# Softmax denominators by block transposes on VectorE in place of DMA, and the MLP of a batch directly behind its attention

## The chip, the cores and the metric

The kernel runs on one core of one Trainium2 chip. The metric is the device time of one execution in microseconds (us), the median of several runs. A core has TensorE (matrix products, the profile's PE; its weight loads are PEld), VectorE (DVE), ScalarE (ACT), GpSimd (POOL) and SyncE (SP, which here only starts transfers). Each engine works through its own queue in order. Queues wait for one another by semaphores.

## The reference, cut to what matters

```python
# B, H, S, D = 8, 8, 576, 64;  d_model = 512, d_ff = 2048
scores = q @ k.T / sqrt(D) + decay            # decay from cumulative log f
scores = where(causal, -1e9, scores)
attn   = softmax(scores);  o = attn @ v       # per batch and head
x = o.transpose(0, 2, 1, 3).reshape(B * S, H * D)
out = gelu_tanh(x @ w_in) @ w_out
```

The kernel works on transposed scores, so the softmax denominator of a query comes out of the attn-V product as one more output row: extra columns of the stationary operand hold the decay weights. Four heads are one item, and a batch has two items.

## The kernel before

The parts (cuts marked):

```python
psS: 2 tiles of 2 PSUM banks    # scores, and up-projection
psO: 1 tile of 2 PSUM banks     # po, attn-V of one head
psM: 2 tiles of 1 PSUM bank     # pso, down-projection

def attn_out(i, h):
    po = psO.tile([128, 1024], FP32)
    # ... 9 matmuls: 64 rows of numerator, and a denominator row in the other half
    nc.vector.tensor_copy(oT[i % 2][:, h, :], po[:, 256:256 + S])

def den_load(i, h):     # DMA: the denominator row to 16 partitions
def den_spread(i, x):   # reciprocal, DMA to DRAM, DMA broadcast to rb (64 rows per head)
def scale_out(i, x):
    for y in range(2):  # GpSimd, half the partitions each
        nc.gpsimd.tensor_mul(xT[b % 3][s, ...], oT[i % 2][s, 2 * x + y, :], rb[s, :])

def mask(i, r):         # VectorE: causal mask on the diagonal blocks of round r
    nc.vector.tensor_mul(p[...], p[...], utri)

def step(i, j, old, fill, per_round, n=None, out_first=False):
    for r in range(4):
        score_round(i, r)              # TensorE, then exponentials on ScalarE
        attn_out(j, r); den_load(j, r)
        # ... GpSimd casts, VectorE transposes of q and k, den_spread, scale_out
        if r > 0: mask(i, r - 1)
        pull(fill, per_round)          # held down-projection matmuls
        if r == 3: mask(i, 3)          # ...

for b in range(3, B + 1):
    mlp_in(b - 2, ...)                 # up-projection of an older batch
    # ...
    for i in (2 * b, 2 * b + 1):
        step(i, i - 1, i - 2, fill, held // 8, ...)
```

Every step has the scores of one item beside the attn-V of the item before it, and held down-projection matmuls in each round. Attention runs more than one batch ahead of the MLP.

The softmax here doesn't subtract the row's maximum and nothing guards it: scores larger than these inputs give would overflow.

## Time and profile before

| quantity | before |
|---|---|
| time, median of 4 runs | 428.88 us |
| span of the profiled run | 425.9 us |
| first long up-projection burst starts at | 60.0 us |
| second starts at | 136.2 us |
| two steady batches (136.16 to 224.89) | 88.73 us, TensorE busy 84.02 |

The first lines of the profile page give the span, and each engine's busy time and instruction count:

```profile
span 425.9 us, 7272 instructions
PE 355.0 (83%) x2825; PEld 210.9 (50%) x2825; DVE 160.7 (38%) x263; ACT 204.0 (48%) x274; POOL 177.7 (42%) x159
```

The waits view, TensorE only. Each line says who waited for whom: total us, times, longest us.

```profile
PE ps_h L253 <- POOL xT_100 L245: 17.3, 5, 5.5
PE ps_h L253 <- POOL xT_101 L245: 13.2, 1, 13.2
...
PE po L206 <- DVE pt_96 L194: 4.1, 5, 1.1
PE po L206 <- DVE oT_98 L213: 3.5, 1, 3.5
```

The up-projection (L253) loses 32 us to normalised attention output that comes late (a third line, of 1.6 us, is not shown), all but 3.5 us of it before 136 us. Behind those GpSimd multiplies stand the transfers of the denominators: row load, store and broadcast.

From there on TensorE sets the pace: it is busy for 84.02 of the next 88.73 us. One attention round in the timeline (start us, duration us, engine, line, what):

```profile
259.35 0.57 PE L176 MATMUL ps_s<-qT_91,kT_93 32*128 32x448 bf16 x8
259.86 0.86 PE L206 MATMUL po<-pt_96,v_aug_94 128*128 128x256 bf16 x7
260.55 2.11 PE L270 MATMUL pso<-w_out_sb,gT 128*128 128x512 bf16 x9
260.82 0.76 DVE L213 COPY oT_98<-po 128x576 f32<-128x576 f32 x1 [1.55 <-PE po L206]
261.50 0.73 DVE L194 TENSOR_TENSOR pt_97<-pt_97,utri 128x512 bf16<-128x512 bf16 x1
262.59 0.52 PE L176 MATMUL ps_s<-qT_91,kT_93 32*128 32x320 bf16 x16
```

Scores, attn-V and held matmuls follow one another without a hole.

### The profile page before, as it was taken

To read this page: it belongs to the slowest core of one execution; us is meant where nothing else is said; L and a number is where in the kernel's file an instruction comes from. 1 tells how busy PE (TensorE), PEld (TensorE's weight loads), DVE (VectorE), ACT (ScalarE), POOL (GpSimd) and SP (SyncE) were. 2 spreads that over 40 slices of the span, in tenths; PEclk is the share of its full clock that TensorE was granted. 3 is DMA by queue.
4 is the path that set the end of the run, shared out by engine and by line. 5 is a ranking of instruction groups with operands and counts; after the bars stand their busy time and mean duration, and the time that the engine had idled before them with its cause. 6 is when DMAs were issued, how large, how long until landed. Compare 5 with 4: busy or idle time off the path is not lost.

```text
span 425.9 us, 7272 instructions
## 1 busy us (share of the span) xinstructions
PE 355.0 (83%) x2825; PEld 210.9 (50%) x2825; DVE 160.7 (38%) x263; ACT 204.0 (48%) x274; POOL 177.7 (42%) x159
## 2 busy tenths in 40 slices
PE   0577149878806999999889999999899989999996
PEld 0234027434403754575447644764476445766642
DVE  6285301274502136531743164505630774000021
ACT  2656116745301664567545745575557551643300
POOL 2491583242805605770568054812881553600000
PEclk9968659899876999999999999999999999999999
DMA  9999179966771971289137922594310132301021
GB/s 194 219 200 181 60 162 199 204 124 154 178 151 70 230 153 69 79 193 195 55 107 190 199 79 83 156 195 116 108 53 2 56 107 83 83 0 51 25 75 74
DMA packets 94642, 52.31 MB, mean 123 GB/s; under 512 B 44880, under 2 KB 85840, under 8 KB 94608
## 3 DMA queue, kind: packets, MB, share of 16 engines
q1 hardware_dynamic: 87952, 46.47, 46.6%
q0 software_dynamic: 4224, 4.19, 6.2%
q10 hardware_dynamic: 2432, 1.18, 1.4%
q8 instruction: 22, 0.36, 0.4%
q14 instruction: 12, 0.10, 0.1%
HBM read 46.28 MB, written 9.58 MB: 131 GB/s over the span
## 4 chain that ended last, share of the span: by engine, by line
PE 55%; DMA 8%; DVE 6%; issue 4%; SPq 3%; ACT 3%; POOL 1%; DVEq 0%; POOLq 0%; ACTq 0%
PE ps_h L253 26%; PE pso L270 20%; PE po L206 6%; DMA rb<-rrow 3%; PE ps_s L176 3%; DMA rrow<-den 3%; DVE pt_96 L194 2%; ACT pt_96 L185 2%; SPq L116 2%; DVE pt_97 L194 1%; DVE oT_99 L213 1%; DMA den<-oT_98 1%; SPq L104 1%; ACT L185 1%; POOL xT_100 L245 1%
## 5 line engine op out<-in xcount | busy, mean ns | idle before, releaser
L270 PE MATMUL pso<-w_out_sb,gT 128*128 128x512 bf16 x576 | 138.5, 384 | 0.0
L260 ACT ACTIVATE gT<-ps_h 128x576 bf16<-128x576 f32 x128 | 83.2, 650 | 112.8 <-PE ps_h L253 112.8
L253 PEld LDWEIGHTS <-w_in_sb 128*128 128x128 bf16 x1024 | 101.4, 99 | 65.6 <-issue 33.5
L270 PEld LDWEIGHTS <-gT 128*128 128x128 bf16 x576 | 53.2, 99 | 60.5 <-issue 7.7
L185 ACT ACTIVATE pt_97<-ps_s 128x800 bf16<-128x800 f32 (+3 forms) x64 | 50.1, 834 | 48.4 <-PE ps_s L176 40.6
L253 PE MATMUL ps_h<-xT_100,w_in_sb 128*128 128x288 bf16 x384 | 50.8, 294 | 17.3 <-POOL xT_100 L245 17.3
L185 ACT ACTIVATE pt_96<-ps_s 128x800 bf16<-128x800 f32 (+3 forms) x64 | 50.1, 834 | 30.7 <-PE ps_s L176 21.1
L253 PE MATMUL ps_h<-xT_101,w_in_sb 128*128 128x288 bf16 x384 | 51.6, 290 | 13.2 <-POOL xT_101 L245 13.2
L213 DVE COPY oT_99<-po 128x576 f32<-128x576 f32 x32 | 24.1, 753 | 86.9 <-PE po L206 86.8
L274 DVE COPY o_st<-pso 128x512 f32<-128x512 f32 x36 | 24.5, 680 | 70.7 <-PE pso L270 70.5
L213 DVE COPY oT_98<-po 128x576 f32<-128x576 f32 x32 | 24.2, 755 | 39.9 <-PE po L206 39.6
L206 PE MATMUL po<-pt_96,v_aug_94 128*128 128x320 bf16 (+4 forms) x224 | 31.9, 281 | 8.0 <-DVE pt_96 L194 4.1
L206 PE MATMUL po<-pt_97,v_aug_95 128*128 128x320 bf16 (+4 forms) x224 | 29.3, 268 | 5.2 <-DVE pt_97 L194 2.8
L253 PE MATMUL ps_h<-xT_102,w_in_sb 128*128 128x288 bf16 x256 | 32.2, 286 | 1.6 <-POOL xT_102 L245 1.6
L245 POOL TENSOR_TENSOR xT_100<-oT_98,rb 64x576 bf16<-64x576 f32 x12 | 17.2, 1436 | 37.8 <-DMA rb<-rrow 37.3
L245 POOL TENSOR_TENSOR xT_101<-oT_98,rb 64x576 bf16<-64x576 f32 x12 | 16.9, 1408 | 33.6 <-DMA rb<-rrow 28.1
L176 PE MATMUL ps_s<-qT_90,kT_92 32*128 32x400 bf16 (+5 forms) x384 | 22.1, 295 | 10.3 <-DVE kT_92 L137 4.6
L206 PEld LDWEIGHTS <-v_aug_94 128*128 128x128 bf16 x224 | 19.0, 103 | 17.9 <-issue 13.6
L194 DVE TENSOR_TENSOR pt_97<-pt_97,utri 128x512 bf16<-128x512 bf16 (+1 forms) x40 | 27.3, 711 | 0.0
L206 PEld LDWEIGHTS <-v_aug_95 128*128 128x128 bf16 x224 | 18.8, 99 | 15.6 <-issue 11.3
L245 POOL TENSOR_TENSOR xT_101<-oT_99,rb 64x576 bf16<-64x576 f32 x12 | 17.0, 1413 | 22.3 <-DMA rb<-rrow 18.6
L194 DVE TENSOR_TENSOR pt_96<-pt_96,utri 128x512 bf16<-128x512 bf16 (+1 forms) x40 | 25.7, 671 | 0.0
(59 smaller groups left out, 236.0 us busy)
## 6 DMA issues: line engine op xcount, KB each, us to landing
rb<-rrow SPq DMA_DIRECT2D x64, 144.0 KB, 3.0
out_dram<-o_st SPq DMA_DIRECT2D x36, 256.0 KB, 2.2
k_nat_84<-in_k_dram SPq DMA_DIRECT2D x32, 144.0 KB, 4.4
k_nat_85<-in_k_dram SPq DMA_DIRECT2D x32, 144.0 KB, 4.5
v_nat_88<-in_v_dram SPq DMA_DIRECT2D x16, 256.0 KB, 6.3
v_nat_89<-in_v_dram SPq DMA_DIRECT2D x16, 256.0 KB, 5.9
q_nat_82<-in_q_dram SPq DMA_DIRECT2D x28, 144.0 KB, 4.7
q_nat_83<-in_q_dram SPq DMA_DIRECT2D x28, 144.0 KB, 5.2
```

Of the source, the lines that this page charges most:

```text
L104: eng.dma_start(out=dst[i % 2][32 * h:32 * h + 32].rearrange("p a e d -> p a (e d)"), in_=src[b, h0 + h].rearrange("(a p e) d -> p a (e d) ...
L116: nc.sync.dma_start(out=v_nat[b % 2][:n, t, :, :], in_=v[b, :, 128 * t:128 * t + n, :].rearrange("h p d -> p h d"),)
L176: nc.tensor.matmul(tiles[h // 2][:, h % 2, c0:c0 + nq], kk[32 * h:32 * h + 32, 128 * t:128 * t + 128, c], qq[32 * h:32 * h + 32, q0:q0 + n ...
L185: nc.scalar.activation(p[:, 2 * g:2 * g + 2, off:off + n], tiles[g][:, :, 0:n], AF.Exp, scale=scale)
L194: nc.vector.tensor_mul(p[:, :, o:o + w], p[:, :, o:o + w], utri[:, :, :w].to_broadcast([128, 4, w]))
L206: nc.tensor.matmul(po[:, base + s - a:base + z - a], va[:, t, h, :], p[:, h, strip_off[t] + s - 128 * t:strip_off[t] + z - 128 * t], start ...
L213: nc.vector.tensor_copy(oT[i % 2][:, h, :], po[:, 256:256 + S])
L245: nc.gpsimd.tensor_mul(xT[b % 3][s, 2 * u + x, :], oT[i % 2][s, 2 * x + y, :], rb[s, :])
L253: nc.tensor.matmul(ph[:, j, 0:hS], w_in_sb[:, dt, 128 * ft:128 * ft + 128], xT[b % 3][:, dt, hS * j:hS * (j + 1)], start=(dt == 0), stop=( ...
L260: nc.scalar.activation(gT[:, ft, o:o + S].rearrange("p (j n) -> p j n", j=2), ph[:, :, 0:hS], AF.Gelu_apprx_tanh)
L270: nc.tensor.matmul(pso, gT[:, ft, c:c + 128], w_out_sb[:, ft, :], start=(ft == 0), stop=(ft == N_FT - 1))
L274: nc.vector.tensor_copy(st, pso)
```

## The change

It has two intents: no denominator should travel by DMA, and with its delay gone the MLP of a batch can follow its own attention. Its core:

```diff
-        nc.gpsimd.tensor_copy(va[:, :, 1:3, 0:1], w.unsqueeze(3))
+        nc.gpsimd.tensor_copy(va[:, :, 1:3, 0:64:32], w...)   # a denominator row per 32-row block
 def attn_out(i, h):
-        nc.vector.tensor_copy(oT[i % 2][:, h, :], po[:, 256:256 + S])
+        nc.scalar.copy(num[mine, :], po[mine, 256:256 + S])
+        nc.vector.transpose(out=den[mine, :], in_=po[other, 256:256 + S])
+        if y == 1:                                  # second head of a pair
+            nc.vector.reciprocal(rec, den[:, 0:S:32])
+            nc.vector.transpose(out=rb..., in_=rec...to_broadcast([128, S // 32, 32]))
+            nc.gpsimd.tensor_mul(xT[b % 2][:, 2 * u + x, :], num, rb)
-    def den_load ... den_spread ... scale_out ...
 # order, per batch b:
-        for ft in range(N_FT): mlp_in(b - 2, ft)
-        for i in (2b, 2b + 1): step(i, i - 1, i - 2, fill, held // 8)
+        mlp_in(b, ...)
+        pull(fill, 3)
+        step(i, None, fill, 5 + 2 * extra)          # scores alone
+        step(i + 1, i, fill, 5 + extra)             # scores beside attn-V
+        step(None, i + 1, fill, 3)                  # attn-V alone
+        pull(fill, 5)
```

Cut: `mlp_in` takes the first two tiles together and leaves their last input for the end, xT has two buffers in place of three, and the loads of the start are reordered (V in halves, weights earlier).

## The prediction

> **What bounds it now.** The page shows TensorE busy 355.0 of 425.9 us, ScalarE 204.0, GpSimd 177.7, VectorE 160.7. Two regimes:
> - From 132 us on (timeline of TensorE) the kernel is TensorE-bound: a pair of batches takes 88.75 us (starts of the long up-projection bursts at 136.3 and 225.05). Each attention round is scores 0.5, attn-V 0.69, seven or nine down-projection matmuls of 0.216: gapless.
> - Before that it waits. The waits view has TensorE's up-projection waiting 17.3 and 13.2 us for GpSimd's xT multiplies, which wait for the broadcast reciprocals (DMA rb, 132 us in total, mostly harmless). The timeline shows TensorE nearly empty from 42.7 to 60 us and from 117 to 131 us, plus 3.5 us at 105. Each denominator goes through four steps: row load (2.0 to 2.6 us to landing), reciprocal 0.36, store 2.0, broadcast 3.0, queued in order behind loads on SP.
>
> **Removed.** All 160 denominator transfers (9.4 MB of broadcast reads), 64 half-height multiplies of 1.41 us, and 64 PSUM copies of 0.755 us on VectorE.
>
> **Added.** Per head, one ScalarE copy of 64x576 (estimate 0.65 us, from the 128x576 Gelu) and one VectorE transpose of 576 columns from PSUM (estimate 0.77, from the existing 128x576 transposes, 0.75 to 0.78). Per pair: a reciprocal of 18 columns (estimate 0.2), another transpose (0.77), one full-height multiply (1.41). VectorE gains about 2.5 us per batch, ScalarE 5.2; GpSimd loses 5.6. The Trainium skill ("VectorE: DVE Perf Modes", The three transpose paths) says VectorE transposes 32x32 blocks only; that suffices, since a block's first row becomes its first column and the second transpose broadcasts it.
>
> **Moved.** Attention no longer runs one batch ahead under another item's attn-V. Per batch: scores alone, scores with attn-V, attn-V alone, then directly the up-projection. I replayed the queues by hand with the durations above:
> - Scores alone are bound by ScalarE: 1.57 us of exponentials plus 0.5 us turnaround per round, against 1.7 to 2.1 us on TensorE; the table load (1.28) is exposed at its start. 1 to 2.7 us lost per batch.
> - First attn-V of the last step waits for VectorE's masks behind two transposes and reciprocals: 2 to 3 us (now 1.0).
> - attn-V alone: one PSUM buffer, round 1.76 us (seen in today's last step), TensorE has 1.4: 1 to 2 us.
> - Last chain transpose, reciprocal, transpose, multiply: 3.2 us, mostly covered by 12 early up-projection matmuls and five held ones: 0.3 to 1 us.
>
> So a batch period goes from 44.4 to about 47.5 us: +3 x 7 = +21 us. Start: the first up-projection ends near 60 us instead of 78, and the second batch's 17 us of waits vanish: -32 us in all, since attention then waits on engines, not DMA.
>
> **Prediction.** 429.5 - 12 = 417 us, range 402 to 431. Faster by over 2%: 0.58; within 2%: 0.32; slower by over 2%: 0.10.
>
> **Right or wrong, in the profile.** Waits view: TensorE waits on xT below 10 us in total (32 now); no rb DMA. By-form groups: VectorE PSUM transpose near 0.77 us, ScalarE copy near 0.65. Timeline: first long up-projection burst starts at 42 to 46 us; period 46 to 49 us; new waits of TensorE on ScalarE (score PSUM), VectorE masks and po totalling 30 to 50 us; ScalarE busy near 240, VectorE near 180, GpSimd near 135 us.
>
> **What would make it wrong.** Mask and po waits smaller than my replay (held matmuls cover them): 400 to 408. Slower PSUM transposes, late w_out loads at 60 to 70 us, or a TensorE clock that drops in the new gaps (0.59 at 40 to 60 us now): no gain.

## More of the kernel before

One VectorE copy of 0.76 us frees po, and VectorE turns to the mask of the next item at once.

The windows view of two batches: window, its length, then busy us (instructions) of PE, PEld, DVE, ACT and POOL, the granted TensorE clock as a share of full speed, the DMA share and GB/s.

```profile
136.16:224.89 88.73, 84.02 (x706) 50.65 (x704) 39.65 (x61) 50.98 (x68) 42.61 (x36) 1.00 0.58 133
```

## The result

The changed kernel takes 467.15 us (467.03 to 467.66, 4 runs), slower by 8.8%: ratio 1.0884, 95% interval 1.082 to 1.0949. Ratios are the mean time of one kernel's fast runs over that of the other's of the same rounds, so they are not quite the ratios of the medians quoted.

```profile
span 465.6 us, 6954 instructions
PE 373.1 (80%) x2789; PEld 216.9 (47%) x2825; DVE 180.3 (39%) x295; ACT 244.5 (53%) x340; POOL 130.0 (28%) x127
```

The loads of the engines are those forecast (ScalarE near 240, VectorE near 180, GpSimd near 135). So are the costs of single instructions. The groups view: busy us, mean ns of one, then the idle time just before them and what ended it.

```profile
L226 DVE STREAM_TRANSPOSE den<-po 64x576 f32<-64x576 f32 x64 | 49.9, 780 | 83.0 <-ACT num L225 82.8
L225 ACT COPY num<-po 64x576 f32<-64x576 f32 x64 | 40.4, 632 | 93.8 <-PE po L212 93.3
L232 DVE STREAM_TRANSPOSE rb<-rec 128x576 f32<-128x576 f32 x32 | 24.9, 778 | 2.2
L230 DVE RECIPROCAL rec<-den 128x18 f32<-128x18 f32 x32 | 8.6, 268 | 1.1
```

The surprise stands behind the second bar. The transpose L226 does not wait for TensorE's attn-V. It waits for ScalarE's copy, 82.8 us in total. The two readers of po run one after the other.

The waits view:

```profile
DVE den L226 <- ACT num L225: 82.8, 61, 2.2
...
PE po L212 <- DVE den L226: 37.3, 50, 1.6
PE po L212 <- DVE pt_95 L198: 16.5, 16, 1.1
...
PE ps_h L245 <- POOL xT_96 L234: 4.6, 4, 1.4
...
PE ps_h L245 <- POOL xT_97 L234: 3.2, 3, 1.1
```

The 32 us of waits for xT are down to 7.8. In their place TensorE waits 37.3 us for po to be free and 16.5 us, in another 16 waits, for masks (a further line, of 3.2 us, is not shown). Between the second and the fourth long up-projection burst (113.39 to 219.06, a pair of batches, which the experiments are compared by), the two waits are:

```profile
PE po L212 <- DVE den L226: 7.6, 12, 1.1
PE po L212 <- DVE pt_95 L198: 4.2, 4, 1.1
```

The timeline from the last round with scores into the attn-V alone:

```profile
147.60 1.24 PE L263 MATMUL pso<-w_out_sb,gT 128*128 128x512 bf16 x5
147.67 0.63 ACT L225 COPY num<-po 64x576 f32<-64x576 f32 x1
148.34 0.78 DVE L226 STREAM_TRANSPOSE den<-po 64x576 f32<-64x576 f32 x1 [0.66 <-ACT num L225]
149.15 0.27 DVE L230 RECIPROCAL rec<-den 128x18 f32<-128x18 f32 x1
149.17 0.41 PE L212 MATMUL po<-pt_95,v_aug_93 128*128 128x256 bf16 x2 [0.33 <-DVE den L226]
149.45 0.78 DVE L232 STREAM_TRANSPOSE rb<-rec 128x576 f32<-128x576 f32 x1
150.15 2.13 DVE L198 TENSOR_TENSOR pt_95<-pt_95,utri 128x512 bf16<-128x512 bf16 x3
150.37 1.42 POOL L234 TENSOR_TENSOR xT_96<-num,rb 128x576 bf16<-128x576 f32 x1 [4.24 <-DVE rb L232]
150.59 0.43 PE L212 MATMUL po<-pt_95,v_aug_93 128*128 128x128 bf16 x3 [1.02 <-DVE pt_95 L198]
152.13 0.48 PE L212 MATMUL po<-pt_95,v_aug_93 128*128 128x320 bf16 x2 [1.11 <-DVE pt_95 L198]
152.43 1.47 PE L263 MATMUL pso<-w_out_sb,gT 128*128 128x512 bf16 x3
...
154.21 1.46 PE L212 MATMUL po<-pt_95,v_aug_93 128*128 128x256 bf16 x7 [0.32 <-DVE den L226]
```

The three masks of the next item (L198) stand in VectorE's queue behind the transpose (which waits for ScalarE's copy), the reciprocal and the second transpose of this item. Nothing needs those before the up-projection, but the next attn-V needs the masks. This accounts for the first mask wait, 1.02 us. The second, 1.11 us, has another reason: the second transpose has released a GpSimd multiply (150.37 to 151.79), and beside it the three masks take 2.13 us. In e11 below the same three take 1.03 us (from 141.96) with no multiply beside them. TensorE has little to do from 149 to 152 us, and then its work takes twice as long: attn-V 1.46 us in place of 0.84. The windows view of the same stretch (columns as above; the last but two is the granted clock):

```profile
151.00:152.00 1.00, 0.02 (x1) 0.00 (x0) 1.00 (x1) 0.00 (x0) 0.80 (x1) 1.00 0.00 0
152.00:153.00 1.00, 0.87 (x4) 0.45 (x4) 0.28 (x2) 0.30 (x1) 0.00 (x0) 0.54 0.00 0
153.00:154.00 1.00, 0.89 (x3) 0.15 (x1) 0.63 (x1) 0.34 (x1) 0.00 (x0) 0.50 0.00 0
154.00:155.00 1.00, 0.79 (x4) 0.51 (x4) 0.15 (x1) 0.00 (x0) 0.00 (x0) 0.50 0.00 0
155.00:156.00 1.00, 1.00 (x7) 0.61 (x6) 0.00 (x0) 0.30 (x1) 0.00 (x0) 0.75 0.00 0
```

The clock is at half from 152 to some 155.5 us, after the hole. The Trainium skill ("TensorE: Matmul & The Clock Gate", Part 1) describes this: the clock is halved after a window of 3.4 us in which the array was idle, and restored after a busy one. The trace agrees on the half and on the length, about 3.4 us. It differs on the cause: the array was not idle for a whole window. From 149 to 152 us it was busy for 0.84 us, between waits of at most 1.1 us each. The same part of the page tells of a second case, in which short idle times between groups of matmuls, frequent enough, make the clock swing. The trace is nearer to that one.

Two steady batches together, to be set beside the 88.73 us of before:

```profile
113.39:219.06 105.67, 89.29 (x696) 52.37 (x705) 41.73 (x69) 60.40 (x85) 30.82 (x29) 0.97 0.41 90
```

TensorE's idle time in the pair is 105.67 - 89.29 = 16.4 us (4.7 before), and its busy time for the same work is 5.3 us longer.

### The profile page after: what moved, and what is told of

The parts are those of the page before. It is cut to its first block, busy times and chain, and to the rows that moved or that the text cites. A ratio compares the mean times of both kernels' runs of the same rounds, so it can differ in the third digit from the quotient of the medians.

```text
span 465.6 us, 6954 instructions
## 1 busy us (share of the span) xinstructions
PE 373.1 (80%) x2789; PEld 216.9 (47%) x2825; DVE 180.3 (39%) x295; ACT 244.5 (53%) x340; POOL 130.0 (28%) x127
## 4 chain that ended last, share of the span: by engine, by line
PE 53%; DVE 18%; ACT 15%; issue 6%; DMA 3%; POOL 2%; POOLq 0%; SPq 0%; ACTq 0%; DVEq 0%
PE ps_h L245 25%; PE pso L263 14%; PE po L212 10%; DVE den L226 9%; ACT num L225 7%; PE ps_s L180 4%; ACT pt_94 L189 4%; DVE pt_95 L198 3%; ACT pt_95 L189 3%; DVE rb L232 3%; DVE pt_94 L198 2%; POOL xT_96 L234 1%; DMA k_nat_82<-in_k_dram 1%; DMA k_nat_83<-in_k_dram 1%; DMA q_nat_81<-in_q_dram 1%
## 5 line engine op out<-in xcount | busy, mean ns | idle before, releaser
L263 PE MATMUL pso<-w_out_sb,gT 128*128 128x512 bf16 x540 | 140.2, 391 | 1.9 <-issue 0.6
L225 ACT COPY num<-po 64x576 f32<-64x576 f32 x64 | 40.4, 632 | 93.8 <-PE po L212 93.3
L226 DVE STREAM_TRANSPOSE den<-po 64x576 f32<-64x576 f32 x64 | 49.9, 780 | 83.0 <-ACT num L225 82.8
L212 PE MATMUL po<-pt_95,v_aug_93 128*128 128x320 bf16 (+4 forms) x224 | 39.0, 316 | 43.1 <-DVE den L226 26.5
L198 DVE TENSOR_TENSOR pt_94<-pt_94,utri 128x512 bf16<-128x512 bf16 (+1 forms) x40 | 21.8, 565 | 111.3 <-ACT pt_94 L189 110.9
L234 POOL TENSOR_TENSOR xT_97<-num,rb 128x576 bf16<-128x576 f32 x16 | 22.6, 1412 | 144.4 <-DVE rb L232 144.4
L234 POOL TENSOR_TENSOR xT_96<-num,rb 128x576 bf16<-128x576 f32 x16 | 22.6, 1410 | 129.5 <-DVE rb L232 119.0
L212 PEld LDWEIGHTS <-v_aug_93 128*128 128x128 bf16 x224 | 24.3, 115 | 65.0 <-issue 56.8
L212 PE MATMUL po<-pt_94,v_aug_92 128*128 128x320 bf16 (+4 forms) x224 | 30.2, 276 | 15.9 <-DVE den L226 10.8
L180 PE MATMUL ps_s<-qT_88,kT_90 32*128 32x400 bf16 (+5 forms) x384 | 25.2, 295 | 12.2 <-ACT pt_94 L189 6.6
L212 PEld LDWEIGHTS <-v_aug_92 128*128 128x128 bf16 x224 | 20.1, 101 | 27.2 <-issue 20.4
L232 DVE STREAM_TRANSPOSE rb<-rec 128x576 f32<-128x576 f32 x32 | 24.9, 778 | 2.2
L180 PEld LDWEIGHTS <-kT_90 32*128 32x128 bf16 x384 | 10.1, 95 | 30.9 <-issue 24.8
L198 DVE TENSOR_TENSOR pt_95<-pt_95,utri 128x512 bf16<-128x512 bf16 (+1 forms) x40 | 23.1, 609 | 0.0
```

Source lines behind the costliest of these rows:

```text
L180: nc.tensor.matmul(tiles[h // 2][:, h % 2, c0:c0 + nq], kk[32 * h:32 * h + 32, 128 * t:128 * t + 128, c], qq[32 * h:32 * h + 32, q0:q0 + n ...
L198: nc.vector.tensor_mul(p[:, :, o:o + w], p[:, :, o:o + w], utri[:, :, :w].to_broadcast([128, 4, w]))
L212: nc.tensor.matmul(po[:, base + s - a:base + z - a], va[:, t, h, :], p[:, h, strip_off[t] + s - 128 * t:strip_off[t] + z - 128 * t], start ...
L225: nc.scalar.copy(num[mine, :], po[mine, 256:256 + S])
L226: nc.vector.transpose(out=den[mine, :], in_=po[other, 256:256 + S])
L232: nc.vector.transpose(out=rb.rearrange("p (c j) -> p c j", j=32), in_=rec.unsqueeze(2).to_broadcast([128, S // 32, 32]))
```

## The experiments

Fourteen kernels ran (there is no e5 or e6 on record). All gave correct results. The theories, as the expectations name them:

- **A**: the loss is po, held for two readers in a row.
- **B**: the loss is the new order itself, whatever the denominators.
- **C**: the new denominators load VectorE and ScalarE too much wherever they stand.
- **D**, formed after the first four runs: the loss is the masks' place in VectorE's queue, behind the denominators.

The two halves of the change can be had singly, and two repairs can be made in both orders. The medians in us (expectations and edits follow):

| | as the change has it | po freed early by ScalarE | masks first | both |
|---|---|---|---|---|
| old order, new denominators | 444.1 | 438.7 | 409.6 | **400.3** |
| new order, new denominators (the change) | 467.2 | 477.0 | 445.7 | 441.6 |

Old order with the old denominators is the kernel before, 428.9 us. New order with the old denominators took 544.3 us.

### e1: the old order with the new denominators

```diff
 # from the kernel before; attn_out and the two weight columns as in the change
-        den_load, den_spread, scale_out and their calls in step
+        nc.scalar.copy(num[mine, :], po[mine, ...]); nc.vector.transpose(out=den[mine, :], in_=po[other, ...])
+        # ... second head: reciprocal, transpose, one multiply
```

> The order of the kernel before (attention one batch ahead of the MLP, nothing else moved), with only the denominators of the change: ScalarE copy, then two VectorE transposes, multiply by GpSimd. Theory A (the loss is the po accumulator held for two readers in a row, 0.63 us of ScalarE copy and then 0.78 us of VectorE transpose, and it shows only where nothing else fills a round): a round here is 3.2 us, po is held some 1.5 us after attn-V, so the steady period stays near 44 us and the 30 us of DMA waits at the start vanish: 398 to 412 us. Theory B (the new order is what loses, whatever the denominators): the same, about 400. Theory C (the new denominators load VectorE and ScalarE too much wherever they stand): 430 or more.

Measured: 444.14 us, ratio 1.0367 (1.0323 to 1.0411). A and B missed: they said about 400. C's number (430 or more) was met, but its reason falls with e8 and e15 below, where the same denominators take 400 and 410 us in another queue order. Two steady batches took 96.6 us (before 88.7). TensorE waited 6.1 us of them for masks and only 0.4 for po, and the clock was 0.96. So the denominators alone, in the old order, already lose, and the masks are the visible wait. At the start the second burst came at 123.4 us, 12.8 earlier than before, where 30 had been expected.

### e2: the new order, ScalarE alone frees po

```diff
-        nc.scalar.copy(num[mine, :], po[mine, 256:256 + S])
-        nc.vector.transpose(out=den[mine, :], in_=po[other, 256:256 + S])
+        nc.scalar.copy(num[:, y, :], po[:, 256:256 + S])
+        nc.vector.transpose(out=den[mine, :], in_=num[other, y, :])
 # ... and the multiply in two halves of 64 partitions
```

> The changed kernel, but ScalarE copies all 128 rows of po to SBUF and the VectorE transpose reads that copy; po is free after ScalarE alone (same copy duration, 0.63 us), at the price of two half-height GpSimd multiplies per pair in place of one. Theory A: rounds of attn-V alone fall from about 3.05 and 2.45 us to about 1.8, the period from 53.6 to 47 to 49 us, in all 425 to 440 us. Theory B: little changes, over 455 us. Theory C: no change, 467 or slightly more.

Measured: 477.00 us, ratio 1.1132 (1.1083 to 1.1182). Theory A's forecast failed, although its mechanism did what was asked: the waits for po in a pair of batches fell from 7.6 to 0.4 us. But the waits for masks rose from 4.2 to 9.1, those for xT from 2.2 to 5.0, and the clock fell to 0.92. Why the masks grew is seen in its timeline:

```profile
143.21 0.38 DVE L198 TENSOR_TENSOR pt<-pt,utri 128x512 bf16<-128x512 bf16 x1
143.43 2.90 POOL L236 TENSOR_TENSOR xT<-num,rb 64x576 bf16<-64x576 f32 x2 [23.11 <-DVE rb L232]
...
145.05 1.57 DVE L198 TENSOR_TENSOR pt<-pt,utri 128x512 bf16<-128x512 bf16 x1
```

A mask of the same size takes 0.38 us when it starts before GpSimd's multiplies and 1.57 us when it starts within them. The Trainium skill ("Advanced Engine Details and Errata", Miscellaneous Facts, GPSIMD Details) says that GpSimd shares a read and a write interface with VectorE and conflicts with its instructions that have two SBUF inputs, which the masks are. The trace agrees. Two multiplies of half height take twice as long as one of full height (1.41 us each), so they cover twice as many masks.

### e3: the new order, VectorE copies too

```diff
-        nc.scalar.copy(num[mine, :], po[mine, 256:256 + S])
+        nc.vector.tensor_copy(num[mine, :], po[mine, 256:256 + S])
```

> The changed kernel, but VectorE makes the copy as well as the transpose, so that both readers of po stand in one queue and ScalarE has 40 us less to do. Theory A (sum of the two readers counts): po is held 0.76 + 0.78 us, no less than before: 458 to 472 us. A rival, that the copy is late because it queues behind the exponentials on ScalarE, expects below 450 us.

Measured: 471.27 us, ratio 1.1008 (1.0956 to 1.1059), as theory A expected. So the copy's place in ScalarE's queue behind the exponentials is not the loss: the rival had expected below 450.

### e4: the new order with the old denominators

```diff
 # from the changed kernel
+        nc.vector.tensor_copy(oT[i % 2][:, h, :], po[:, 256:256 + S]); den_load(j, r)
+        # den_spread and scale_out one item later; after the last item at once
-        # copy, transposes and reciprocal of the change
```

> The order of the change with the denominators of the kernel before (one 0.755 us VectorE copy frees po; row load, reciprocal, store, broadcast by DMA). Theory A: po is held short, rounds of attn-V alone fall to about 1.8 us, saving some 5 us per batch; but the chain of four DMA steps, some 11 us, now lies open before each up-projection with 2.5 us to cover it, 8 to 9 us per batch lost: 485 to 510 us. Theory B says nothing else; if it came out under 467, the transposes themselves would be the loss (theory C).

Measured: 544.28 us, ratio 1.2692 (1.2635 to 1.275). This is outside the expected range on the slow side. TensorE waited 21.4 us for xT in a pair of batches, at a clock of 0.88. The new order needs the new denominators. The chain of transfers cannot lie open before each up-projection.

### e7: the new order, ScalarE frees po, masks first

```diff
 # from e2
+            todo.append(...)                       # attn_out only copies
             if i is not None and r > 0: mask(i, r - 1)
+            if j is not None and (i is None or 0 < r < 3): den_part()   # transpose, reciprocal, ...
             pull(fill, per_round)
             if i is not None and r == 3: mask(i, 3)
+            if i is not None and j is not None and r == 3: den_part(); den_part()
```

> e2 (new order, ScalarE alone frees po) with VectorE's queue reordered: in each round the causal masks of the next item come before the transposes, reciprocal and broadcast of this one; nothing depends on those transposes until the up-projection. Theory D, formed after e1 and e2 (with po freed, the attn-V of the next item waits for masks that stand in VectorE's queue behind the denominators, and GpSimd's multiplies running at the same time stretch those masks to 1.1 us and more): mask waits of a pair of batches fall from 9.1 to 3 us or less, the clock recovers from 0.92 to 0.97 or more, the pair falls from 110.9 to 96 to 102 us, 430 to 448 us in all. Theory B (the order itself, too little to fill the attention steps): stays over 460.

Measured: 441.56 us, ratio 1.0294 (1.0228 to 1.036), within theory D's range. Mask waits of a pair fell from 9.1 to 0.5 us. The clock recovered to 0.96 only, probably because the chain to the up-projection, now with two half-height multiplies, left waits for xT of 6.7 us (e13 tests this).

### e8: the old order with the same two repairs

```diff
 # from e1: the edit of e2 and the edit of e7
```

> The same two changes in the order of the kernel before: ScalarE copies po whole and frees it, the transposes follow the masks in VectorE's queue. Theory D with A: the pair of batches falls from 96.6 us (e1) to 87 to 90 us, as before (88.7), and the waits for DMA at the start stay away, so the second up-projection burst starts near 105 us (before 136, e1 123): 392 to 408 us. If VectorE or ScalarE were simply overloaded by the new denominators (theory C), 425 or more.

Measured: 400.29 us, ratio 0.9331 (0.9278 to 0.9384): 6.7% faster than the kernel before, and the best kernel of this study. Two steady batches, windows view:

```profile
115.91:201.32 85.41, 83.42 (x705) 50.78 (x704) 43.97 (x69) 59.74 (x84) 42.35 (x36) 1.00 0.50 112
```

Its only listed TensorE wait in that window is 2.0 us on ScalarE. The engines do the same denominators as in e1, so theory C falls. The masks are as slow as in e1 (0.697 us on the mean against 0.694, 128x512), yet TensorE no longer waits for them there. So in the old order their place in the queue explains the waits, and not their length. The second burst started at 115.9 us. It was expected near 105, so the start gained 20 us and not 31.

### e9: po as two tiles of one bank

```diff
-        po = psO.tile([128, 1024], FP32, ...)
+        po = [psO.tile([128, 512], FP32, ...) for z in range(2)]
-        nc.scalar.copy(num[mine, :], ...); nc.vector.transpose(out=den[mine, :], ...)
+        nc.scalar.copy(num[mine, 0:256], po[0][mine, 0:256])
+        nc.vector.transpose(out=den[mine, 256:S], in_=po[1][other, 0:S - 256])
+        nc.scalar.copy(num[mine, 256:S], po[1][mine, 0:S - 256])
+        nc.vector.transpose(out=den[mine, 0:256], in_=po[0][other, 0:256])
```

> The changed kernel with po as two tiles of one PSUM bank each: ScalarE copies the first bank while VectorE transposes the second, then they swap, so the two readers overlap; the data read is the same, in twice as many instructions. Theory A (the wait of the transpose for the copy is the program's, because both read one PSUM tile, and not the chip's): the transpose of the second bank starts with the copy, po is held about 1.0 us in place of 1.45, rounds of attn-V alone fall by 0.3 to 0.5 us and the whole to 450 to 462 us. If the readers could not overlap on the chip, each would stretch and nothing be gained: 467 or more.

Measured: 439.46 us, ratio 1.0256 (1.0183 to 1.0328), 28 us under the changed kernel and better than expected. The timeline of one head, from its first transpose on:

```profile
193.93 0.51 DVE L226 STREAM_TRANSPOSE den<-po 64x320 f32<-64x320 f32 x1 [1.76 <-PE po L212]
194.37 0.40 DVE L228 STREAM_TRANSPOSE den<-po 64x256 f32<-64x256 f32 x1
194.48 0.42 ACT L227 COPY num<-po 64x320 f32<-64x320 f32 x1 [0.93 <-DVE den L226]
```

The first transpose now waits for TensorE, where the one of the change waits for ScalarE, and a copy and a transpose overlap from 194.48 to 194.77. So the wait in the change was one that the program had put between two readers of one PSUM tile; here too the second copy waits for the transpose of its own tile (last line). ScalarE and VectorE can read PSUM at once when each has its own tile. Whether they could share one tile, no run shows. The halves cost more than the whole, 0.79 and 0.94 us per head against 0.63 and 0.78. Waits for po in a pair fell from 7.6 to 1.9 us. The masks stayed at 4.2 us and the clock at 0.95.

### e10: the old order, ScalarE frees po, masks where the change has them

```diff
 # from e1: the edit of e2
```

> The fourth cell of the table for the old order: ScalarE alone frees po (as in the 400.3 us run), but the transposes stand in VectorE's queue where the change put them, ahead of the next item's masks (as in the 444.1 us run). If the masks' place is what matters here (theory D): 425 to 440 us, with over 5 us of mask waits of TensorE in a pair of batches. If freeing po early is what matters (theory A): 400 to 412 us.

Measured: 438.67 us, ratio 1.0224 (1.0188 to 1.026): theory D's case. Mask waits in a pair were 6.7 us, the clock 0.96, the pair 96.2 us.

### e11: the new order, masks first and nothing else

```diff
         nc.scalar.copy(num[mine, :], po[mine, 256:256 + S])
+        for m in masks:               # rounds (), 0, 1, (2 and 3)
+            mask(*m)
         nc.vector.transpose(out=den[mine, :], in_=po[other, 256:256 + S])
```

> The changed kernel with one thing moved: in each round VectorE's queue has the next item's masks before the transpose of this item's denominators. po still has its two readers in a row and is now held for the masks as well. It completes the table for the new order (467 neither, 477 po freed early, 441.6 both). If the two repairs add up: mask waits of a pair fall by about 4 us and po waits rise by as much, 458 to 472 us. If the place of the masks alone were the cause: about 440 us.

Measured: 445.72 us, ratio 1.0382 (1.033 to 1.0434). It is 21 us under the changed kernel, nearer to the second reading (about 440) than to the first (458 to 472). Mask waits of a pair went to zero, po waits rose from 7.6 only to 9.4, and the clock stood at 1.00. The move takes the masks out from behind the denominators and, for the most part, from beside the multiply. In the new order no run parts the two.

### e14: the held matmuls moved to the attn-V alone

```diff
-                step(i, None, fill, 5 + 2 * extra)
-                step(i + 1, i, fill, 5 + extra)
-                step(None, i + 1, fill, 3)
+                step(i, None, fill, 2 + 2 * extra)
+                step(i + 1, i, fill, 4 + extra)
+                step(None, i + 1, fill, 7)
```

> The changed kernel with the same number of held down-projection matmuls per batch, but moved from the rounds of scores alone (5 or 7 down to 2 or 4) and of scores with attn-V (5 or 6 down to 4 or 5) into the rounds of attn-V alone (3 up to 7). The first are bound by ScalarE at about 2.1 us either way; the last hold po for 2.4 us and leave TensorE empty for some 1 us each. If the loss is only that work stood in the wrong rounds: po waits of a pair fall from 7.6 to below 3 us, the clock rises to 0.99, 440 to 455 us. If the new order has too little work for its twelve rounds whatever the places: 460 or more.

Measured: 472.53 us, ratio 1.1012 (1.0962 to 1.1061), in the range of the second reading (460 or more). Waits for po did fall, to 3.3 us, but waits for ScalarE's exponentials rose from 1.6 to 4.4, the masks stayed at 4.2, and the clock fell from 0.97 to 0.92. Beside e11 it shows what the clock costs. The windows view of two steady batches of e11:

```profile
108.07:208.05 99.98, 86.66 (x705) 51.39 (x704) 40.40 (x69) 60.44 (x85) 30.76 (x29) 1.00 0.44 95
```

and of e14:

```profile
113.11:221.32 108.21, 95.44 (x706) 53.96 (x704) 41.70 (x69) 60.58 (x85) 30.76 (x29) 0.92 0.40 88
```

TensorE idles 13.3 us in the one and 12.8 us in the other (window less busy time). The same matmuls are busy 8.8 us longer in the second, where the clock is 0.92. My reading is that the cost of idle time depends on how it is bunched: in e14 the mask waits still stand close together. The two kernels differ in more than that, and no run changes the bunching alone.

### e13: the end of the chain split over two engines

```diff
 # from e7: last pair of a batch
-                nc.gpsimd.tensor_mul(xT..., num[m, z, :], rb[m, :])
+                eng = nc.vector if (z == 1 and last pair) else nc.gpsimd
+                eng.tensor_mul(xT..., num[m, z, :], rb[m, :])
```

> The 441.6 us kernel (new order, ScalarE frees po, masks first) with the last pair's two half-height multiplies of a batch made side by side by GpSimd and VectorE, so that the chain between the last attn-V and the up-projection is 1.4 us or more shorter. If the open chain is what is left of the new order's loss: the waits of TensorE for xT fall from 6.7 to below 3 us in a pair of batches, and the kernel to 425 to 433 us. If the loss lies in the rounds themselves (too little for TensorE to do beside ScalarE's exponentials): 436 us or more.

Measured: 422.93 us, ratio 0.9857 (0.981 to 0.9905), better than expected, and the best of the new order, though within 2% of the kernel before. Waits for xT fell only to 4.7 us, more than the expected 3, but the clock of the steady pair went from 0.96 to 1.00 and its busy time from 90.8 to 87.1 us.

### e12: an earlier weight load for the best kernel

```diff
 # from e8
         load_qk(2)
-        load_v(1)
+        w_in_dmas = [load_w_in(c) for c in range(4)]
         step(1, 0, None, none, 0, n=2)
-        for c in range(4): load_w_in(c)
+        v1 = load_v(1); after(v1[0], w_in_dmas[2])   # and make_vaug(2) after mlp_in(0)
```

> The 400.3 us kernel with the first MLP weights loaded one step earlier and the second batch's V after them, because its first up-projection waited 5.7 us for that weight load. Expected: that wait vanishes, the first long burst starts near 48 us in place of 53, 394 to 399 us. If the transfers only change places and the next ones come late, 400 or more.

Measured: 400.80 us, ratio 0.9343 (0.9308 to 0.9377): nothing gained. The 5.7 us wait for the weights is gone, and TensorE waits 8.8 us for GpSimd's multiplies instead (3.9 in e8). Either the late weights had hidden that wait or the new order of loads made it; this was not looked into.

### e15: the old order, masks first and nothing else

```diff
 # from e1: the edit of e11
```

> The old order with the change's denominators (444.1 us run) and only the masks moved ahead of the transposes in VectorE's queue; po still has two readers in a row. It completes the table for the old order (444.1 neither, 438.7 po freed early, 400.3 both). If the place of the masks alone costs the 44 us: 398 to 408 us, clock of a steady pair back at 1.00, mask waits below 1 us. If po must also be freed early: 415 to 435 us, with po waits of 4 us or more in a pair.

Measured: 409.63 us, ratio 0.9541 (0.9498 to 0.9584), a little over the expected range for the masks alone. The clock of the steady pair is 1.00, mask waits are gone, po waits are 1.2 us. So of the 44 us between e1 and e8, 34.5 are the masks' place, and some 9 are left for freeing po.

### e16: the new order with po in two tiles and masks first

```diff
 # from e9: the edit of e11
```

> The new order with po in two tiles that are read side by side (439.5 us run) and the masks ahead of the transposes (445.7 us run). If the two repairs are separate and add up: 415 to 425 us, clock 0.99 or more in a steady pair, po waits below 4 us; still over the 400 us of the old order with repaired queues, because scores alone stay bound by ScalarE. If both only removed the same clock drop: 436 to 446 us.

Measured: 425.65 us, ratio 0.9922 (0.9872 to 0.9973). The total is just over the expected range. The two repairs nearly add up (41.5 us, where singly they gave 27.7 and 21.4), though po waits of 6.9 us per pair stayed above the expected 4. It only comes level with the kernel before, and 25 us behind the old order with repaired queues.

## Why the prediction was wrong

It said 417 us, range 402 to 431. Measured were 467.15, some 50 us more. Point by point:

- **Costs of single instructions: right.** Copy 0.632 us (0.65 forecast), transpose 0.780 (0.77), second transpose 0.778 (0.77), reciprocal 0.268 (0.2), multiply 1.41. The skill's statement that VectorE transposes in blocks of 32 ("VectorE: DVE Perf Modes", The three transpose paths) carried as the prediction used it: the results are correct.
- **DMA waits: right.** Waits for xT are 7.8 us (below 10 forecast).
- **"attn-V alone: one PSUM buffer, round 1.76 us": the step that failed first.** The figure is the round of the kernel before, in whose last step one copy of 0.76 us frees po. The change gives po two readers, and the estimate has no time for the second. They run one after the other, 0.63 + 0.78 us, and rounds are about 2.4 us at full clock (e11) and 3.05 us at the half clock of the start. e9 shows the wait to be the program's, and worth 28 us with its share at the start. With this and the masks repaired (e16) the new order takes 425.65 us, inside the predicted range: the two account for 41.5 of the 50 us.
- **Clock: named as a risk, costed at nothing.** The prediction put the wait for masks at 2 to 3 us per batch, and it was 2.1 (4.2 per pair). But two such waits and one for po, close together, were followed by half the clock for 3.4 us (152 to 155.5 us). Moving the masks alone (e11) took the clock to 1.00 and gave 21 us. e14 against e11 shows 8.8 us of longer matmuls in a pair at equal idle time.
- **"So a batch period goes from 44.4 to about 47.5 us": mis-sized.** It was 105.67 / 2 = 52.8 us. TensorE's new waits, put at 30 to 50 us in all, were 63.6 (37.3 for po, 19.7 for masks, 6.6 for exponentials). Over seven periods, (52.8 - 47.5) x 7 = 37 us of the miss.
- **"-32 us in all" at the start: mis-sized.** The first burst was to start at 42 to 46 us and started at 57.8 (60.0 before), in part because the rounds of attn-V alone took 3.05 us each (1.49 of it attn-V at half clock) and the first of the four, with mask waits, 5.0. From the first attn-V to the last (39.62 to 50.72) that is 11.1 us where three rounds of 1.76 make 5.3; the other 6 to 10 us of the delay were not traced. The first up-projection ended at 72.7 us and not near 60: 13 us of the miss.
- **The direction of each half.** I took the new denominators for a gain in themselves. In the old order they lost 15 us (e1), because of the queue on VectorE (e15 moves the masks alone and is 34.5 us faster). With the queue repaired they gain 28 us (e8).
- **The new order: "+21 us", right in sign, too small.** With both queues repaired and the same denominators, the new order (441.6) is 41 us behind the old (400.3). With the chain to the up-projection shortened too it is 23 us behind (e13). The rest is in the trace of e13, but no run here parts it: in a pair TensorE still waits 4.7 us for xT, 1.6 for exponentials and 0.5 each for masks and po (e8: 2.0 for exponentials alone), and it is busy for 87.1 us against 83.4.

What stays open: how much of the start's loss is the half clock and how much the masks that GpSimd stretches there, how much of the masks' 21 us in the new order is their place and how much the multiply beside them, and how the 23 us that the new order still costs divide.

## What to carry to other kernels

When a change adds work to an in-order queue, look at what stands behind it there: 1.8 us of denominators that nobody needed yet, and the GpSimd multiply that they release, made the masks late that TensorE needed at once. Moving the masks ahead gave 34 us in the old order and 21 in the new. Two engines that read one accumulator are parallel only if the program's dependencies say so, so look at what the second reader waits for before giving it no time of its own. Cost TensorE's waits with the clock: here three short ones within 3 us were followed by half the clock for about as long again, while e11, with as much idle time as e14 in a pair, kept it at 1.00.

## What the Trainium skill lacked or had wrong

- "TensorE: Matmul & The Clock Gate" gives a figure for the drop of the clock only for an idle window, 3.4 us in Part 1 and some 3 us in its advice on idle gaps. For its second case, short idle times that come often, it has no threshold. Here 0.84 us of matmul work within 149 to 152 us, between waits of at most 1.1 us, did not prevent the drop. In e11, waits of up to 1.4 us spread over the rounds kept it at 1.00.
- "VectorE: DVE Perf Modes" gives one duration for VectorE's transpose, for 128x128 bf16. From PSUM in fp32, 64 partitions, the runs show 0.780 us for 576 columns, 0.514 for 320 and 0.424 for 256.
